# Parked output weights return after the q products, a fifth block of them is parked, and more of V stays on the chip

## The chip, the cores and the metric

The kernel runs on one core of a Trainium2 chip. The metric is device time in microseconds (us) of one execution. The core has the engines PE (TensorE, matrix products into PSUM), DVE (VectorE), ACT (ScalarE), POOL (GpSimd) and SP (SyncE, which issues the transfers from HBM). PEld is PE's loading of weights, which overlaps its products.

## The reference

Four residual layers over x of 4 x 1 x 512: attention, gated unit, attention, gated unit. Both attention layers use the same weights and caches, and so do both gated units.

```python
def _A_ref(x, k_cache, v_cache, wq, wo):          # Hq 32, Hkv 8, Dh 128, Sk 8192
    W = min(4096, max(256, Sk // 4))              # 2048: only the last 2048 keys count
    q = (x @ wq).reshape(B, Sq, Hq, Dh).transpose(0, 2, 1, 3)
    k = jnp.repeat(k_cache[:, :, Sk - W:, :], rep, axis=1)   # rep 4
    v = jnp.repeat(v_cache[:, :, Sk - W:, :], rep, axis=1)
    p = _softmax(jnp.einsum("bhqd,bhkd->bhqk", q, k) * (Dh ** -0.5), axis=-1)
    o = jnp.einsum("bhqk,bhkd->bhqd", p, v)
    return o.transpose(0, 2, 1, 3).reshape(B, Sq, Hq * Dh) @ wo

def _B_ref(x, w_gate, w_up, w_down):              # F 1792
    return (sigmoid(x @ w_gate) * (x @ w_up)) @ w_down

x = x + _A_ref(_layernorm(x), ...)
x = x + _B_ref(_layernorm(x), ...)
x = x + _A_ref(_layernorm(x), ...)
x = x + _B_ref(_layernorm(x), ...)
```

All inputs are bf16. K and V of the window are 16 MiB each.

## The kernel before

**Stages.** The layers are numbered 0 to 3. Layer 0 loads wq, K of all heads and V head by head. K is transposed on PE (L741) and copied back to its place by ACT and DVE (L751), so that layer 2 finds it on the chip. Per head: scores (L764), maximum (L773), exp (L786), a block transpose of the weights (L792, L797), their spreading over the four batches (DVE L822, in layer 2 also ACT L829), the reciprocal of their sum (L837, L841), the product with V (PV: L864 in the wide form, whose column groups L880 adds up, L922 in the plain form), its scaling (omul, L933) and the product with the head's rows of wo (L985, for the last heads L896 or L947). Layer 0 takes the heads in the order 1 to 6, 0, 7, layer 2 in the order 0 to 7. The gated units load w_up, w_gate (L1152) and w_down (L1228 in layer 1, L1225 in layer 3).

**Places.** On-chip memory is dealt out in units of 128 x 256 bf16 (64 KB over all partitions). The places are `arena` ("ar", 75 units), `wo_sb` ("ws", 64 units, 8 per head for wo), `kt` ("kt", 256 units, 32 per head for K), `side` ("sx") and the small `pb` and `pt`. The table `WHERE` gives each load its places. V of a head has 32 units. `VKEEP` names the unit from which V of a head stays on the chip between layers 0 and 2: for head 7 it is unit 26, so that six units are kept and 26 are loaded again. In layer 2, V of heads 2 to 7 goes to places in `kt` that K of heads 0 to 5 leaves free, each as soon as the scores of that head are done.

**Parking.** In layers 1 and 2 some units of `wo_sb` are wanted for other weights. `stash(0)` copies four blocks of four units (ws 8 to 23, DVE L1032) into PSUM banks 1, 2, 0 and 3. Then w_gate, a piece of w_down and two pieces of wq are loaded into these units. `stash(1)` copies the blocks back (ACT L1028). It stands ahead of `project_q` (L704, the q products of layer 2) in the program.

**Row sum's bank.** PSUM bank 7 (`WB`) gathers the wo products of most heads (L985): four strips of 32 rows, of which each strip's first 16 rows are written. It is set to zero once at the start. At the end of an attention layer ACT and DVE copy it as hi and lo parts (L998, L1004), and eight products with the 0/1 tile `ofbb` (L1011, w_turn) sum its rows and turn them; w_early (L1017) adds this to x.

**Order.** Each operation is entered with the tokens that it reads and writes, its PSUM banks and a planned time. `_schedule` places the operations of each engine by these planned times, `_assign_sync` adds the waits. So moving or adding an operation can change the order on the other engines. SP issues the transfers strictly in the order of the program, each once its places are free.

Of the kernel before, what the change touches and what calls it, by code (L numbers as in the profile page):

```python
# [268 lines left out]
def build(nc, A_x, A_k, A_v, A_wq, A_wo, B_wg, B_wu, B_wd, out):  # L269
# [3 lines left out]
    NB, SQ, D = A_x.shape  # L273
    _, HKV, SK, DH = A_k.shape
# [15 lines left out]
    NR = NB * REP  # L290
# [3 lines left out]
    WOH = REP * D  # L294
# [10 lines left out]
    AHEAD = 2  # L305
    NWR = {0: HKV - 1, 2: HKV - 2}
    WIDE = {0: {0: 4, 1: 4, 2: 4, 3: 4, 4: 4, 5: 4, 6: 2}, 2: {2: 2, 3: 2, 4: 2, 5: 2}}
    VKEEP = {0: 24, 7: 26}
    HEADS1 = list(range(1, HKV - 1)) + [0, HKV - 1]
    HEADS2 = list(range(HKV))  # L310

# [27 lines left out]
    with es:  # L339
# [3 lines left out]
        kt = sb("kt", [128, HKV * NB * BLK], BF16)  # L343
        wo_sb = sb("wo_sb", [128, HKV * WOH], BF16)
# [12 lines left out]
        pb = sb("pb", [128, 4 * UNIT], BF16)  # L357
# [4 lines left out]
        tin = sb("tin", [128, 32], F32)  # L362
# [9 lines left out]
        ofb, ofr = (lambda t: (t[:, 0:NB], t[:, NB:2 * NB]))(sb("ofbr", [128, 2 * NB], F32))  # L372
        onr = sb("onr", [128, 4 * NR], BF16)
# [3 lines left out]
        rowq, ofbb, ones_b = (lambda t: (t[:, 0:NR], t[:, NR:NR + NB], t[:, NR + NB:]))(sb("rqb", [128, NR + NB + 2], BF16))  # L377
# [16 lines left out]
        ps = es.enter_context(nc.psum_tensor("ps", [128, 8, 512], F32))  # L394
# [5 lines left out]
        P = _Plan()  # L400
# [9 lines left out]
        def blk_tok(s):  # L410
            return tuple((s[0], u) for u in range(s[1], s[1] + s[2]))
# [12 lines left out]
        def ar(u, n):  # L424
            return ("ar", u, n)

        def sx(u, n):
            return ("sx", u, n)

        WHERE = {}  # L430
        for n in range(HKV - 1):
            WHERE["V0_%d" % HEADS1[n]] = [ar(MAIN - UHEAD if n % 2 == 0 else 0, UHEAD)]
        WHERE["V0_%d" % (HKV - 1)] = [ar(0, 16), ar(16, 10), ar(30, 6)]
        WHERE["u01"], WHERE["g01"] = ar(52, 2 * GU), ar(38, 2 * GU)
        PT3 = ("kt", 187, 4)
        WHERE.update({
            "g23_1": ("ws", 8, 2 * GU), "u23_1": ar(0, 2 * GU),
            "d0_1": ar(14, 8), "d4_1": ar(22, 8), "d8_1": ar(36, 2), "d9_1": ("ws", 22, 2), "d10_1": ("pb", 0, 4),
            "d12_1": ("pt", 4, 4),
            "q01": [("ws", 8, 8), ar(0, 14), ar(14, 4), ("ws", 16, 6)],  # L440
            "V2_0": [ar(18, 12), ar(36, 2), sx(0, 8), sx(8, 2), ar(66, 8)],
            "V2_1": [sx(10, NS - 10), ar(0, 11)],
            "V2_6": [("kt", 128, 16), ("kt", 144, 16)],
            "V2_7": [("kt", 160, 16), ("kt", 176, 10), ar(30, 6)],
            "g23_3": ar(0, 2 * GU), "u23_3": sx(0, 2 * GU),
            "d0_3": ar(14, 8), "d4_3": ("kt", 192, 8), "d8_3": ("kt", 200, 8), "d12_3": sx(14, 4),
        })
# [7 lines left out]
        def c_dve(n, rate=None):  # L455
            return tm["dve_fix"] + n * (tm["dve_f32"] if rate is None else rate)
# [14 lines left out]
        def load_v(L, h):  # L471
# [3 lines left out]
            for s in WHERE["V%d_%d" % (L, h)]:  # L475
# [16 lines left out]
             r=[("ones_f",)], w=[("ident_f",)])  # L492
        P.op("gpsimd", "ident_b", 200.0, lambda g: g.tensor_copy(ident_r[:, :].rearrange("p (r x) -> p r x", r=4),
                                                                   ident_f[:, :].unsqueeze(1).broadcast_to([128, 4, 128])),
             r=[("ident_f",)], w=[("ident_b",)])
# [9 lines left out]
        def e_rowq(v):  # L505
            with nc.allow_low_precision("zeros and ones"):
# [8 lines left out]
             r=[("ident_f",)], w=[("perm",)])  # L515
        P.op("vector", "ofb", c_dve(128),
             lambda v: v.tensor_reduce(ofb[:, :], ident_f[:, :].rearrange("p (s b) -> p b s", b=NB), AXX, ALU.add),
             r=[("ident_f",)], w=[("ofb",)])
        P.op("vector", "ofr", c_dve(128),
             lambda v: v.tensor_reduce(ofr[:, :], ident_f[:, :].rearrange("p (r y) -> p r y", r=REP), AXX, ALU.add),  # L520
             r=[("ident_f",)], w=[("ofr",)])
        P.op("vector", "ofbb", c_dve(NB), lambda v: v.tensor_copy(ofbb[:, :], ofb[:, :]), r=[("ofb",)], w=[("ofbb",)])

        P.op("vector", "own", c_dve(16),
             lambda v: v.tensor_reduce(tin[:, 0:REP], rowq[:, :].rearrange("p (b r) -> p r b", b=NB), AXX, ALU.add),
             r=[("rowq",)], w=[("tin",)])
        P.op("vector", "same0", c_dve(32),
             lambda v: v.tensor_copy(tout[:, :], eye32[:, :]), r=[("eye32",)], w=[("tout",)])
        P.op("vector", "same1", c_dve(16),
# [2 lines left out]
             r=[("tin",), ("tout",)], w=[("tout",)])  # L532
        P.op("vector", "same2", c_dve(32),
             lambda v: v.tensor_scalar(same[:, :], tout[:, :], -1.0e30, 1.0e30, ALU.mult, ALU.add),
             r=[("tout",)], w=[("same",)])
# [3 lines left out]
        WB = 7  # L539
# [8 lines left out]
        def emit_xT_in(t):  # L548
            last = None
            for c in range(NC):  # L550
# [4 lines left out]
             w=[("psx",)], banks=(MB,))  # L555
        P.op("vector", "xT_cp", c_dve(NX), lambda v: v.tensor_copy(xT[:, :], bankb(MB)[:, 0:NX]),
             r=[("psx",)], w=[("xT",)], banks=(MB,))
# [134 lines left out]
        def project_q(L, pieces, pieces_last):  # L692
            if not L:
                return project_first(pieces, pieces_last)
            prev, toks, seen = [], {0: [], 1: []}, set()
            HB = HQ // 2
            for n, (ap, tk, ktc, q0, q1) in enumerate(pieces):
                on = sorted(set(q // HB for q in range(q0, q1)))
                first = [max(q0, i * HB) for i in on if i not in seen]
                seen.update(on)  # L700

                def e_q(pe, ap=ap, ktc=ktc, q0=q0, q1=q1, first=first):
                    for q in range(q0, q1):
                        last = pe.matmul(ps[:, QB + q // HB, q % HB * NB:(q % HB + 1) * NB],  # L704
                                         ap[:, (q - q0) * 128:(q - q0 + 1) * 128],
                                         xn[:, ktc * (NB + 1):ktc * (NB + 1) + NB],
                                         start=(q in first), stop=(ktc == pieces_last), skip_group_check=True)
                    return last
                prev = [P.op("tensor", "qproj%d_%d" % (L, n), tm["pe_pair"] * (q1 - q0), e_q,
                             r=list(tk) + [("xn",)], w=[("psq", n)], banks=tuple(QB + i for i in on), order=prev)]  # L710
                for i in on:
                    toks[i].append(("psq", n))
            mc = means(L, tq, cs_q, HQ)
            for i in range(2):
                tv = tq[:, i * HB * NB:(i + 1) * HB * NB]
                P.op("vector", "q_mean%d_%d" % (L, i), c_dve(HB * NB),
                     lambda v, i=i, tv=tv: v.tensor_tensor(tv, ps[:, QB + i, 0:HB * NB], tv, ALU.subtract),
                     r=toks[i] + [mc], w=[("qm", i)], banks=(QB + i,))
                P.op("vector", "q_evac%d_%d" % (L, i), c_dve(HB * NB),
                     lambda v, i=i, tv=tv: v.tensor_tensor(  # L720
                         qs[:, 28:28 + HKV * NB * STRIP].rearrange("p (h b s) -> p h b s", h=HKV, b=NB)[:, 4 * i:4 * i + 4, :, 0:REP],
                         tv.rearrange("p (h r b) -> p h b r", h=HKV // 2, r=REP),
                         rstd[:, :].unsqueeze(1).unsqueeze(3).broadcast_to([128, HKV // 2, NB, REP]), ALU.mult),
                     r=[("qm", i), ("rstd",)], w=[("qs1",)] if i else [("qs",)])
# [177 lines left out]
        def pv_wo(L, n, h, pbk, pieces, prev=()):  # L902
# [8 lines left out]
            for s, j0 in () if wide else pieces:  # L911
                def e_pv(pe, s=s, j0=j0):
                    last = None
                    j1 = j0 + s[2] * UNIT // 128
                    for j in range(j0, j1):
# [13 lines left out]
                             r=blk_tok(s) + pk + (("pa", kp),), w=[("pso", obk, j0)], banks=(obk,), order=prev)]  # L929
# [12 lines left out]
            if n == HKV - 1:  # L942
                def e_wo(pe):
                    last = None
                    for c in range(NC):
# [7 lines left out]
                     r=[("wo", h), ("on", k2)], w=[("psl", obk)], banks=(obk,))  # L953
# [28 lines left out]
            def e_wo(pe):  # L982
                last = None
                for j in range(4):
                    last = pe.matmul(ps[32 * j:32 * j + NR, WB, 0:D], onr[:, j * NR:(j + 1) * NR],  # L985
                                     wo_sb[:, h * WOH + j * D:h * WOH + (j + 1) * D],
                                     start=(n == 0), stop=(n == NWR[L] - 1), skip_group_check=True)
                return last
# [29 lines left out]
                 r=[("pswt",), ("xT",)], w=[("xT",)], banks=(MB,))  # L1018

        GB, UB, YB = 0, 1, 2  # L1020
        STASH = ((8, 3), (12, 0), (16, 1), (20, 2))

        def stash(back):
            for u, b in STASH if back else STASH[1:] + STASH[:1]:
                at = blk_ap(("ws", u, 4))
                r, w = [("wo", u * UNIT // WOH)], [("st", b)]
                if back:
                    P.op("scalar", "back%d" % u, 1010.0, lambda a, b=b, at=at: a.copy(at, bankb(b)), r=w,  # L1028
                         w=r + list(blk_tok(("ws", u, 4))), banks=(b,))
                else:  # L1030
                    P.op("vector", "stash%d" % u, 620.0,
                         lambda v, b=b, at=at: v.tensor_scalar(ps[:, b, :].bitcast(I32), at.bitcast(I32), 0, None, ALU.bitwise_or),  # L1032
                         r=r, w=w + [("pst", b), ("pss", b)] + list(blk_tok(("ws", u, 4))), banks=(b,))

        gkeep = {}

# [94 lines left out]
        def glu(L, last_layer):  # L1131
# [76 lines left out]

            parts = [(fc, min(NFC, fc + 4)) for fc in range(0, NFC, 4)]
            if not last_layer:  # L1210
                parts[2:] = [(8, 9), (9, 10), (10, 12), (12, 14)]
            for fc0, fc1 in parts:
                s = load_d(L, fc0, fc1)

# [101 lines left out]
        for w in WHERE["q01"]:  # L1316
# [6 lines left out]
                    streamed.append((blk_ap(t), blk_tok(t), ktc, q0, q1))  # L1323
            u0 += w[2]
        assert u0 == HQ
        stash(1)
        project_q(2, kept_q + streamed, 1)
        vs2 = {}
        SB2, TB2 = [3, 0], [1, 2]

# [10 lines left out]
        turns = []  # L1341
        for n, h in enumerate(HEADS2):
            turns.append(scores(2, n, h, SB2[n % 2], TB2[n % 2]))
            if n + 1 < HKV:
                vs2[HEADS2[n + 1]] = load_v(2, HEADS2[n + 1])
            if n >= AHEAD:
                v2_head(n - AHEAD)
            weights(2, n, h, TB2[n % 2])
# [67 lines left out]
```

## Time and profile before

| | |
|---|---|
| median of 3 runs | 174.94 us (174.22 to 174.97) |
| profiled execution | 174.91 us |
| its span | 173.2 us |
| mean granted clock of PE | 0.819 |
| PE, DVE, ACT, POOL busy | 78%, 58%, 44%, 4% |
| read from HBM | 69.08 MB, 399 GB/s over the span |

The page of the profile has the busy shares of the engines, the span in 40 slices with the granted clock of PE (`PEclk`, tenths of full speed), the share of the 16 transfer rings that is busy (`DMA`) and the GB/s, then the queues and the chain of work that ended last. Beside the page there are views of the trace: the chain of waits in order of time, the timeline of single instructions, the transfers with the time from issue to landing, and the busy times by windows. A bracket at the end of a line of the timeline gives the engine's idle time before it and what ended that. Times in the trace count from the start of the span.

### The profile page before, as it was taken

Reading aid. Unit: us, or ns where it says so; the run is one execution under the profiler, and the core shown is the slowest. Engines: PE = TensorE matmul, PEld = TensorE weight load, DVE = VectorE, ACT = ScalarE, POOL = GpSimd, SP = SyncE. Lnnn points to the kernel's source line nnn. Section 1 sums busy time; section 2 is a strip of 40 time slices with the busy share of each in tenths; the row PEclk is TensorE's granted clock in tenths of the full one; section 3 lists DMA queues with packets and bytes.
Section 4 is the critical chain, followed back from the end, with each engine's and each line's share of the span. In section 5 each row is a group of like instructions: output and inputs, shape, how many; then the busy total and the mean of one; then the engine's idle time right before and its main releaser. Section 6 shows DMA issues by size and latency. Waiting matters only on the chain.

```text
span 173.2 us, 4888 instructions
## 1 busy us (share of the span) xinstructions
PE 135.6 (78%) x2178; PEld 98.5 (57%) x2178; DVE 100.0 (58%) x251; ACT 76.4 (44%) x133; POOL 7.0 (4%) x18
## 2 busy tenths in 40 slices
PE   0394599899798778997988785757887999868894
PEld 0292298657466465564764465756523766556782
DVE  7444015986838677695697643114187988854260
ACT  2064208848477547466292122023524644564110
POOL 5200000000000000000000000200200000100020
PEclk9999656999999999999999655555576999985555
DMA  5999999999999999999999999999999999999970
GB/s 183 424 429 418 417 424 431 424 408 446 428 412 429 407 433 435 409 437 419 429 415 418 395 391 411 409 393 413 414 432 435 422 416 414 420 418 419 413 310 29
DMA packets 9648, 69.39 MB, mean 401 GB/s; under 512 B 1048, under 2 KB 2204, under 8 KB 6172
## 3 DMA queue, kind: packets, MB, share of 16 engines
q1 hardware_dynamic: 9620, 69.08, 96.2%
q8 instruction: 17, 0.28, 0.6%
q14 instruction: 3, 0.02, 0.0%
q10 hardware_dynamic: 8, 0.00, 0.0%
HBM read 69.08 MB, written 0.00 MB: 399 GB/s over the span
## 4 chain that ended last, share of the span: by engine, by line
DMA 57%; PE 28%; DVE 6%; ACT 5%; issue 1%; SPq 1%; DVEq 0%; ACTq 0%
DMA arena<-in_A_v_cache_dram 32%; DMA kt<-in_A_v_cache_dram 11%; DMA arena<-in_A_wq_dram 10%; PE ps L764 5%; PE ps L864 5%; DMA wo_sb<-in_A_wq_dram 4%; PE ps L1152 4%; PE ps L741 4%; PE ps L673 2%; PE ps L922 2%; ACT pb L786 1%; ACT pt L829 1%; ACT wo_sb L1028 1%; PE ps L1225 1%; SPq L464 1%
## 5 line engine op out<-in xcount | busy, mean ns | idle before, releaser
L751 ACT COPY kt<-ps 128x1024 bf16<-128x1024 bf16 x40 | 39.1, 1018 | 26.0 <-PE ps L741 25.8
L741 PE MATMUL ps<-ident_r,kt 128*128 128x128 bf16 x512 | 38.6, 232 | 4.9 <-DMA kt<-in_A_k_cache_dram 2.7
L741 PEld LDWEIGHTS ps<-ident_r,kt 128*128 128x128 bf16 x512 | 33.1, 106 | 11.7 <-issue 4.4
L751 DVE COPY kt<-ps 128x1024 bf16<-128x1024 bf16 x24 | 29.2, 1215 | 12.9 <-PE ps L741 12.7
L764 PE MATMUL ps<-kt,qs 128*32 128x512 bf16 x256 | 19.3, 426 | 1.7 <-ACT pb L786 1.0
L822 DVE TENSOR_TENSOR pt<-ps,ofbr 128x1024 bf16<-128x1024 f32 (+1 forms) x15 | 15.5, 1030 | 3.3 <-PE ps L797 3.2
L864 PE MATMUL ps<-arena,pt 128*64 128x512 bf16 (+1 forms) x128 | 13.4, 391 | 4.6 <-DMA arena<-in_A_v_cache_dram 4.6
L773 DVE TENSOR_REDUCE nmz<-ps 128x1 f32<-128x512 f32 x16 | 11.0, 687 | 6.4 <-PE ps L764 6.3
L792 DVE STREAM_TRANSPOSE pb<-pb 128x512 bf16<-128x512 bf16 x16 | 11.3, 708 | 5.0 <-ACT pb L786 4.9
L786 ACT ACTIVATE pb<-ps,nmz 128x512 bf16<-128x512 f32 x16 | 11.1, 694 | 5.8 <-DVE nmz L783 5.7
L829 ACT ACTIVATE pt<-ps,ofbr 128x96 bf16<-128x96 f32 x28 | 7.2, 341 | 10.3 <-PE ps L797 10.3
L864 PEld LDWEIGHTS ps<-arena,pt 128*64 128x64 bf16 (+1 forms) x128 | 6.0, 117 | 10.1 <-DMA arena<-in_A_v_cache_dram 6.0
L764 PEld LDWEIGHTS ps<-kt,qs 128*32 128x32 bf16 x256 | 5.9, 102 | 8.0 <-ACT pb L786 1.9
L873 ACT COPY arena<-ps 128x512 f32<-128x512 f32 (+1 forms) x7 | 3.9, 555 | 14.1 <-PE ps L864 14.1
L837 PE MATMUL ps<-rowf,nmz 128*128 128x16 f32 x32 | 6.7, 285 | 2.8 <-DVE pt L822 2.6
L837 PEld LDWEIGHTS ps<-rowf,nmz 128*128 128x128 f32 x32 | 5.2, 203 | 5.8 <-DVE pt L822 4.1
L880 PEld LDWEIGHTS ps<-arena 128*128 128x128 f32 x52 | 6.7, 201 | 2.1 <-ACT arena L873 1.6
L880 PE MATMUL ps<-arena 128*128 128x16 f32 x52 | 7.4, 273 | 0.7 <-ACT arena L873 0.2
L1152 PE MATMUL ps<-xn,arena 128*128 128x5 bf16 (+1 forms) x168 | 6.2, 172 | 2.0 <-DMA arena<-in_B_w_up_dram 1.1
L1152 PEld LDWEIGHTS ps<-xn,arena 128*128 128x128 bf16 x168 | 6.2, 118 | 2.2 <-DMA arena<-in_B_w_up_dram 1.2
L1028 ACT COPY wo_sb<-ps 128x1024 bf16<-128x1024 bf16 x4 | 4.0, 1012 | 7.6 <-DMA wo_sb<-in_A_wq_dram 7.5
L635 POOL TENSOR_TENSOR rs<-pt,rs 128x4 f32<-128x4 f32 x3 | 3.0, 1015 | 107.0 <-DVE pt L631 107.0
(165 smaller groups left out, 159.9 us busy)
## 6 DMA issues: line engine op xcount, KB each, us to landing
kt<-in_A_k_cache_dram SPq DMA_DIRECT2D x8, 2048.0 KB, 24.7
arena<-in_A_v_cache_dram SPq DMA_DIRECT2D x7, 2048.0 KB, 20.3
kt<-in_A_v_cache_dram SPq DMA_DIRECT2D x3, 2048.0 KB, 14.6
kt<-in_A_v_cache_dram SPq DMA_DIRECT2D x5, 1024.0 KB, 18.5
wo_sb<-in_A_wo_dram SPq DMA_DIRECT2D x8, 512.0 KB, 25.4
kt<-in_A_wq_dram SPq DMA_DIRECT2D x1, 2048.0 KB, 11.7
side<-in_A_wq_dram SPq DMA_DIRECT2D x1, 1984.0 KB, 15.8
arena<-in_B_w_up_dram SPq DMA_DIRECT2D x2, 896.0 KB, 7.8
```

Of the source, the lines that this page charges most:

```text
L741: last = pe.transpose(bankb(bank)[:, (v * NB + q) * 128:(v * NB + q + 1) * 128], kt[:, c0:c0 + 128], ident_b[:, :])
L751: return (e.tensor_copy if ev == "vector" else e.copy)(to, fr)
L764: last = pe.matmul(ps[32 * b:32 * b + 32, sbk, 0:CB * 128], qs[:, q0:q0 + 32], blk_ap(kblk(h, b))[:, c * CB * 128:(c + 1) * CB * 128], sta ...
L773: lambda v: v.tensor_reduce(nmv, ps[:, sbk, 0:CB * 128], AXX, ALU.max, negate=True),
L786: o = a.activation(pbuf[:, :], ps[:, sbk, 0:CB * 128], ACTF.Exp, bias=gv, scale=1.0, accum_out=zv)
L792: P.op("vector", "ptr%d_%d" % (L, h), 650.0, lambda v: v.transpose(turned[:, :], pbuf[:, :]), r=[("pb", 0), ("pb", 1)], w=[("pb", 2), ("pb ...
L822: lambda v: v.tensor_tensor(pv4[:, 0:nj], spread(tbk, nj).unsqueeze(2).broadcast_to([128, nj, NB, REP]), ofb[:, :].unsqueeze(1).unsqueeze( ...
L829: last = a.mul(pv4[:, nj:NJ4, b, :], spread(MB, NJ4 - nj), ofb[:, b:b + 1])
L837: lambda pe: pe.matmul(ps[:, tbk, CB * NQ:CB * NQ + NR], zv.broadcast_to([128, 128]), rowf[:, :], start=True, stop=True),
L864: last = pe.matmul(ps[rows * g:rows * (g + 1), bank, 0:wide * 128].rearrange("p (c d) -> p c d", c=wide), ptv[:, w0:w0 + rows], v, start=( ...
L880: last = pe.matmul(ps[:, out[0], out[1]:out[1] + NR], part[:, c * 128:(c + 1) * 128], ey[wide][:, c * NR:(c + 1) * NR], start=(c == 0), st ...
L1152: last = pe.matmul(ps[:, bank, fc * wid:(fc + 1) * wid], cols[:, fc - g0, :], xn[:, ktc * (NB + 1):ktc * (NB + 1) + wid], start=(ktc == 0 ...
```

## The change

1. `VKEEP` of head 7 goes from 26 to 22: ten units of its V are kept in `arena` (26 to 35) between the attention layers, and 22 are loaded again. In both layers the second piece of V of head 7 has 6 units, and the third, kept one has 10.
2. A fifth block of four units (ws 24 to 27) is parked in bank 7 after the row sum of layer 0 has been read from it, and comes back behind the exp of the first head of layer 2.
3. `stash(1)` stands behind `project_q`. The q products of layer 2 thus read the wq pieces in `wo_sb` as they were loaded, and the copies back wait for these products; before, the copies came between the loads and the products.
4. Since bank 7 now holds parked weights in all rows, the first wo product of layer 2 writes 32 rows of the first three strips, and one more product starts the fourth strip; `ofbb` is made from a 0/1 tile (`own`) whose ones stand only at the rows that count.
5. The places of w_down in layer 1 (pieces of 4, 3, 1, 2, 2 and 2 row blocks instead of 4, 4, 1, 1, 2 and 2), of wq in layer 2 (three pieces instead of four) and of the first V of layer 2 move.

The order that results on the engines: in layer 0 PE has 44 PV products of head 7 ahead of w_turn and 20 behind it (32 and 32 before). In layer 2 the scores of head 0 stand behind all q products (before: ahead of the last 12), and those of heads 0 to 2 stand together; for head 7, 20 products with kept V, 32 with the first loaded piece and 12 with the second (12, 32 and 20 before). DVE has one instruction more (the fifth parking, behind L1004), ACT one more copy, which stands behind the first exp of layer 2. Further on ACT has the exp of head 3 ahead of the spreading of head 2.

```diff
-    VKEEP = {0: 24, 7: 26}
+    VKEEP = {0: 24, 7: 22}
...
-        WHERE["V0_%d" % (HKV - 1)] = [ar(0, 16), ar(16, 10), ar(30, 6)]
+        WHERE["V0_%d" % (HKV - 1)] = [ar(0, 16), ar(16, 6), ar(26, 10)]
...
-            "d0_1": ar(14, 8), "d4_1": ar(22, 8), "d8_1": ar(36, 2), "d9_1": ("ws", 22, 2), "d10_1": ("pb", 0, 4),
+            "d0_1": ar(14, 8), "d4_1": ("ws", 22, 6), "d7_1": ar(36, 2), "d8_1": ar(22, 4), "d10_1": ("pb", 0, 4),
             "d12_1": ("pt", 4, 4),
-            "q01": [("ws", 8, 8), ar(0, 14), ar(14, 4), ("ws", 16, 6)],
-            "V2_0": [ar(18, 12), ar(36, 2), sx(0, 8), sx(8, 2), ar(66, 8)],
+            "q01": [("ws", 8, 10), ar(0, 14), ("ws", 18, 8)],
+            "V2_0": [ar(14, 12), ar(36, 2), sx(0, 8), sx(8, 2), ar(66, 8)],
...
-            "V2_7": [("kt", 160, 16), ("kt", 176, 10), ar(30, 6)],
+            "V2_7": [("kt", 160, 16), ("kt", 176, 6), ar(26, 10)],
...
-        P.op("vector", "ofbb", c_dve(NB), lambda v: v.tensor_copy(ofbb[:, :], ofb[:, :]), r=[("ofb",)], w=[("ofbb",)])
...
+        P.op("vector", "ofbb", c_dve(NB), lambda v: v.tensor_copy(ofbb[:, :], tin[:, 0:NB]), r=[("tin",)], w=[("ofbb",)])
...
                 for j in range(4):
-                    last = pe.matmul(ps[32 * j:32 * j + NR, WB, 0:D], onr[:, j * NR:(j + 1) * NR],
+                    rows = 2 * NR if L and n == 0 and j < 3 else NR
+                    if L and n == 0 and j == 3:
+                        pe.matmul(ps[96:128, WB, 0:D], onr[:, 2 * NR:4 * NR], wo_sb[:, h * WOH:h * WOH + D], start=True,
+                                  stop=False, skip_group_check=True)
+                    last = pe.matmul(ps[32 * j:32 * j + rows, WB, 0:D], onr[:, j * NR:j * NR + rows],
...
-        STASH = ((8, 3), (12, 0), (16, 1), (20, 2))
-
-        def stash(back):
-            for u, b in STASH if back else STASH[1:] + STASH[:1]:
+        STASH = ((8, 3), (12, 0), (16, 1), (20, 2), (24, WB))
+
+        def stash(back, at_last=False):
+            for u, b in (STASH[4:] if at_last else STASH[:4]) if back else STASH[1:4] + STASH[:1] + STASH[4:]:
                 at = blk_ap(("ws", u, 4))
                 r, w = [("wo", u * UNIT // WOH)], [("st", b)]
                 if back:
                     P.op("scalar", "back%d" % u, 1010.0, lambda a, b=b, at=at: a.copy(at, bankb(b)), r=w,
-                         w=r + list(blk_tok(("ws", u, 4))), banks=(b,))
+                         w=r + list(blk_tok(("ws", u, 4))), banks=(b,),
+                         order=[o for o in P.ops if o.name == "sexp2_%d" % HEADS2[0]])
                 else:
                     P.op("vector", "stash%d" % u, 620.0,
                          lambda v, b=b, at=at: v.tensor_scalar(ps[:, b, :].bitcast(I32), at.bitcast(I32), 0, None, ALU.bitwise_or),
-                         r=r, w=w + [("pst", b), ("pss", b)] + list(blk_tok(("ws", u, 4))), banks=(b,))
+                         r=r, w=w + [("pst", b), ("pss", b)] + list(blk_tok(("ws", u, 4))) + [("psw", n) for n in range(HKV)] * (b == WB),
+                         banks=(b,))
...
-                parts[2:] = [(8, 9), (9, 10), (10, 12), (12, 14)]
+                parts[1:] = [(4, 7), (7, 8), (8, 10), (10, 12), (12, 14)]
...
-        stash(1)
-        project_q(2, kept_q + streamed, 1)
+        project_q(2, kept_q + streamed, 1)
+        stash(1)
...
             turns.append(scores(2, n, h, SB2[n % 2], TB2[n % 2]))
+            if n == 0:
+                stash(1, True)
```

## The prediction

> **What bounds the kernel now.** I read the page first (clock, transfers, chain), then the chain of waits in order of time, then the timeline of the last stage, the transfers with their time to landing, and the windows over the end.
>
> The page: granted clock and transfer share in 40 slices of 4.33 us, queues, chain by engine.
> ```profile
> PEclk9999656999999999999999655555576999985555
> DMA  5999999999999999999999999999999999999970
> ...
> q1 hardware_dynamic: 9620, 69.08, 96.2%
> q8 instruction: 17, 0.28, 0.6%
> ...
> DMA 57%; PE 28%; DVE 6%; ACT 5%; issue 1%; SPq 1%; DVEq 0%; ACTq 0%
> ```
> The transfers are busy from the first slice to the last but two. 69.08 MB must come in, and the engines work in their shadow.
>
> The chain of waits, in order of time (start, us, what):
> ```profile
> 111.90 7.61 DMA wo_sb<-in_A_wq_dram
> ...
> 119.54 1.02 ACT wo_sb L1028
> ...
> 120.58 1.02 ACT wo_sb L1028
> ...
> 121.65 1.56 PE ps L704 x52
> ...
> 143.17 18.37 DMA kt<-in_A_v_cache_dram
> ...
> 161.58 0.73 PE ps L922 x20
> ```
> The copies back (L1028) do stand on this chain, but the chain then goes through a transfer issued at 143.17 that lands only 18.37 us later: it had stood in a long queue. What the engines win before that gets the last V in no sooner.
>
> The transfers (times, KB, us from issue to landing) and the end of the timeline:
> ```profile
> kt<-in_A_v_cache_dram SPq DMA_DIRECT2D x1, 640.0 KB, 18.4
> ...
> pb<-in_B_w_down_dram SPq DMA_DIRECT2D x1, 256.0 KB, 10.2
> pt<-in_B_w_down_dram SPq DMA_DIRECT2D x1, 256.0 KB, 10.4
> ```
> ```profile
> 161.58 0.61 PEld L922 LDWEIGHTS ps<-kt 128*128 128x128 bf16 x20 [0.40 <-DMA kt<-in_A_v_cache_dram]
> 161.58 0.72 PE L922 MATMUL ps<-kt 128*128 128x32 bf16 x20 [0.30 <-DMA kt<-in_A_v_cache_dram]
> ...
> 169.63 0.34 PEld L1225 LDWEIGHTS ps<-kt,pt 128*25 128x25 bf16 x16 [0.18 <-DMA kt<-in_B_w_down_dram]
> 170.26 0.13 PEld L1225 LDWEIGHTS ps<-side,pt 128*25 128x25 bf16 x8 [0.29 <-DMA side<-in_B_w_down_dram]
> 170.26 0.40 PE L1225 MATMUL ps<-side,pt 128*25 128x128 bf16 x8
> ```
> The last 20 PV products wait for the last V, and the last two groups of the down projection wait for the last weights (0.18 and 0.29 us). So the end is set by the last landing, near 170.2; PE alone could be 0.47 us (0.18 + 0.29) earlier.
>
> The windows over the end (us; busy of PE, PEld, DVE, ACT, POOL; clock; transfer share; GB/s):
> ```profile
> 166.00:166.50 0.50, 0.50 (x21) 0.50 (x19) 0.32 (x2) 0.00 (x0) 0.50 (x1) 0.50 1.04 393
> ...
> 169.50:170.00 0.50, 0.50 (x27) 0.34 (x16) 0.00 (x0) 0.00 (x0) 0.00 (x0) 0.50 0.21 61
> ```
> The 16 rings do not end together: the share falls from 1.04 to 0.21 over 3.5 us. The slowest ring sets the last landing.
>
> **The change part by part.** The profiled execution took 174.91 us (span 173.2 and 1.71 around it), 0.03 under the median 174.94.
>
> Bytes. V of head 7 is streamed in the second attention layer for 22 units instead of 26; four units of 128 x 256 bf16 are 262,144 bytes. From 140 to 160 us the windows show 419, 410, 419 and 417 GB/s, mean 416: 0.63 us. The other sizes change, their sum does not. The Trainium skill (DMA: Bandwidth & Descriptors, section Bandwidth) puts the HBM side at about 358 GB/s per core; by that figure the bytes would be 0.73 us, an estimate, and the sum 0.1 lower; the trace sustains 416 here and decides.
>
> One transfer fewer (wq in three pieces, not four). The pb and pt pieces, issued at 107.33 and 107.81, land at 117.53 and 118.21: 0.68 apart, where 256 KB at 416 GB/s are 0.63. So about 0.05 us each; between 0 and 0.1, I take 0.05.
>
> Sum on the transfers: 0.63 + 0.05 = 0.68 us, all before or at V of head 7, so each later landing moves by that.
>
> PE at the end. The 32 products at 160.27 end at 161.28; now the last piece lands near 160.9, so the wait of 0.30 goes. Twelve products follow instead of 20: 8 x 0.036 (0.72 / 20) = 0.29 less. The eight move to the kept group (near 157.2), ahead of the second half of head 6; that half landed just before its products start at 157.55, with the row sum (L837, 0.61) now written earlier, so I take nothing for them; at worst 0.29 comes back. PE gains 0.59 (0.30 at worst), and had 0.47 to spare: 1.06 (0.77) against 0.68. The transfers stay last.
>
> The fifth parking (stash24, DVE). The nearest row is the fourth, 0.67 us at 97.84. It must follow w_lo (L1004, ends 104.45) and goes 104.46 to 105.13. Queued behind it on DVE are w_early (was 104.99, 0.14 later) and omul0_7, which waits for PE until 105.86. PE now does 12 of the later 32 PV products ahead of w_turn, in its idle 0.54 us before 104.60, so omul0_7 comes about 0.35 sooner. None of it lasts: the next stages wait for u and w_down transfers (113.00, then 114.76 to 118.28). Without that cover it would cost 0.67.
>
> SP's queue. The second w_down piece now goes to parked places and waits for stash24 (105.13); w_down began at 105.54 before, so that is no later. Behind it stand the other w_down pieces and wq. The last wq piece waits for the second w_down group's products (about 116.1; was issued at 115.75), and the first V of layer 2 for the fourth's (about 117.2; was 116.24). These land 7.6 and 9.4 us after issue, queued behind others, so a delay of 0.4 to 1.0 is hidden: 0.
>
> Copies back. Before, two (119.54 to 121.60) held the first wq products, and two (123.38 to 125.44) the last 12. Now products wait for landings alone; the last landing stays near 115.75 + 7.6 = 123.35, as the bytes up to there are the same. S of head 0, now behind all q products on PE, starts near 123.9, as before (123.89), so the place for V of head 2 comes free at 125.83 again. Even if not: the V pieces issued at 123.02 and before land up to 9.7 us after that, so the rings have work to 132.7, and a slip of a few us starves none; past that each us would count in full. Copies of units 16 and 20 run to about 126.0 on ACT; the exp of head 0 began at 127.67, so 1.7 us cover them. The fifth copy (1.01) follows that exp, 128.45 to 129.47; the weights of head 0 (L829) began at 129.73: covered by 0.26, and with no cover at most 1.01 on head 0. The first WO of the layer has one product more, about 0.15 us (0.60 / 4). ACT takes exp of head 3 ahead of the weights of head 2 (0.69 + 0.19 later at worst). All this is ahead of PV waits on transfers at 150.10, 152.58 and 155.21; the weights for the last were ready at 151.79, 3.4 us early. So 0.
>
> Setup (ofbb from another tile): the same DVE instruction one place later, near 3.4 us, where the first K is still on its way: 0. The other transfers that were cut anew (V of head 7 in layer 0, w_down, first V of layer 2) keep their number and bytes: 0. Total: 174.91 - 0.68 = 174.23.
>
> **The rivals.**
>
> Forecast: the last landing moves by 0.68, 174.2. For it: the waits at 161.58, 169.63 and 170.26. Own range 173.9 to 174.6.
>
> A ring step, either way. The page counts 17 instruction fetches, 0.28 MB, so 16.5 KB each; a ring moves 416 / 16 = 26 GB/s, so each fetch delays its ring by 0.63 us. One more or fewer on the slowest ring makes 174.9 or 173.6. For it: rings that end 3.5 us apart, and the three runs (174.97, 174.94, 174.22), which differ by about one such step.
>
> PE becomes the bound. If the longer kept group pushes head 6's half and the later chain so that PE gains nothing, only the spare 0.47 is won: 174.44. It decides once PE gains under 0.21; my worst was 0.30.
>
> Slower: the half clock. The clock is 0.5 from 98 to 127, 1.0 for one stretch, 0.5 again from 131 to 134, then 1.0. S at half takes 1.90 per head, 1.05 at full; 32 PV products of L864 1.90 against 1.24. So a head loses about 1.5 us, or some 1.7 us in 3.4 us of PE work. If the changed order keeps the clock at half through three further such stretches after 134, 5.1 us are lost against the 3.4 of cover at head 6: 174.23 + 1.7 = 175.9. Up to two stretches it costs nothing. For it: PE drops back at 131; against: S of heads 0 to 2 now stand together, so PE idles less there. The Trainium skill (TensorE: Matmul & The Clock Gate, Part 1) says that half rate is the default, that about 3.4 us of sustained activity releases it, and that the window runs free, so that the phase differs from run to run. By that rule the drop at 131 could be longer or absent; the trace agrees as far as a drop of about 3 us goes.
>
> The change does not do what it says: the kept places overwritten and V streamed anyway would be 174.9; the written transfers show 384 KB, so next to nothing.
>
> **How the numbers follow.** A measurement of this kernel tells about 0.5%, 0.87 us: under 174.07 is faster, over 175.81 slower. Forecast 0.50, of which 0.20 below 174.07; ring step down 0.20 (faster), up 0.10 (same); PE bound 0.12 (same); clock 0.08 (slower). Faster 0.40, same 0.30 + 0.10 + 0.12 = 0.52, slower 0.08. The range goes from 173.5 (a step, and the upper price of the dropped transfer) to 175.0 (the step up); it leaves out the clock and the tails.
>
> **What would show it.** Right: 68.8 MB in q1; the last V transfer 384 KB, landing near 160.9, 12 products after it with no wait; the last w_down landing near 169.6, still waited for; no L1028 in the chain; rate unchanged. Wrong: a slice of transfers under 9 between 20 and 160 us; PE not waiting at the end; a half clock from 134 to 150; S of head 0 well after 123.9.

## The result, and the profile after

The changed kernel takes 174.17 us in the median of 22 runs (173.62 to 175.15), the kernel before 174.75 beside it (174.21 to 175.29). The ratio is 0.9971, with a 95% interval of 0.9959 to 0.9984: faster by 0.3%, less than one measurement of this kernel tells from no change. The forecast was 174.2. The profiled execution took 174.00 us, 0.91 under the one before, which is more than the medians moved (0.58). One run further down, of pad448 with 176.92 us, was in a slow state and is left out of its median.

From the page: granted clock and transfer share in 40 slices, the two queues, the chain by engine.
```profile
PEclk9999656999999999999999755555567899995555
DMA  5999999999999999999999999999999999999980
...
q1 hardware_dynamic: 9476, 68.82, 96.4%
q8 instruction: 17, 0.28, 0.6%
...
DMA 53%; PE 31%; DVE 9%; ACT 3%; issue 2%; SPq 1%; DVEq 0%; ACTq 0%
```
0.26 MB less in q1, the same number of instruction fetches, no slice under 9 between the first and the last two. But the transfers' share of the chain fell from 57% to 53%, and PE's and DVE's rose. The chain of waits, in order of time (start, us, what), shows where:
```profile
116.81 6.81 DMA wo_sb<-in_A_wq_dram
123.67 0.59 PE ps L703 x16
...
149.53 0.40 PE ps L836 x2
...
160.07 1.21 PE ps L921 x44
```
No copy back (L1031 now) is left in it, and no transfer either after 123.67: the last V, which carried 18.37 us of the chain before, is gone from it. From the products of q to the end, 46 us, the chain is engines alone in this profile. It is close: V of head 5 landed at 149.52, only 0.33 before its products began (149.85), and in a second profile of the same kernel (control, below) the chain goes through that landing.

The end of the timeline (start, us, engine, line and operation; in brackets the wait before it and what ended it):
```profile
157.21 0.93 PEld L921 LDWEIGHTS ps<-pt,kt 128*128 128x128 bf16 x32 [0.15 <-DMA kt<-in_A_v_cache_dram]
...
159.93 1.33 PE L921 MATMUL ps<-kt 128*128 128x32 bf16 x44
...
168.19 0.13 PEld L1230 LDWEIGHTS ps<-arena,pt 128*25 128x25 bf16 x7 [0.34 <-issue]
...
169.35 0.13 PEld L1230 LDWEIGHTS ps<-side,pt 128*25 128x25 bf16 x8 [0.19 <-DMA side<-in_B_w_down_dram]
169.36 0.40 PE L1230 MATMUL ps<-side,pt 128*25 128x128 bf16 x8
```
The 32 and 12 products of head 7 run as one group of 44 with no wait (0.30 before). The last group waits 0.19 for its weights (0.29 before), and a new stall of 0.34 stands in the middle of the first group of the down projection, put down to no releaser. The last V transfer, among the transfers (KB, us from issue to landing), and the windows over the end (us; busy of PE, PEld, DVE, ACT, POOL; clock; transfer share; GB/s):
```profile
kt<-in_A_v_cache_dram SPq DMA_DIRECT2D x1, 384.0 KB, 17.2
```
```profile
166.00:166.50 0.50, 0.50 (x21) 0.50 (x19) 0.22 (x1) 0.17 (x1) 0.00 (x0) 0.50 0.72 287
...
169.00:169.50 0.50, 0.50 (x27) 0.30 (x15) 0.00 (x0) 0.00 (x0) 0.00 (x0) 0.50 0.12 33
```
The queue thins out 0.9 us sooner: 0.72 at 166 where it was 1.04, and the last landing, by the records of the landings, is 169.32 (170.23 before).

### The profile page after: what moved, and what is told of

Same layout as the page of the kernel before. It is cut to its first block, busy times and chain, and to the rows that moved or that the text cites. A ratio compares the mean times of both kernels' runs of the same rounds, so it can differ in the third digit from the quotient of the medians.

```text
span 172.3 us, 4893 instructions
## 1 busy us (share of the span) xinstructions
PE 134.8 (78%) x2179; PEld 98.2 (57%) x2179; DVE 100.9 (59%) x252; ACT 77.3 (45%) x134; POOL 7.0 (4%) x18
## 3 DMA queue, kind: packets, MB, share of 16 engines
q1 hardware_dynamic: 9476, 68.82, 96.4%
HBM read 68.82 MB, written 0.00 MB: 400 GB/s over the span
## 4 chain that ended last, share of the span: by engine, by line
DMA 53%; PE 31%; DVE 9%; ACT 3%; issue 2%; SPq 1%; DVEq 0%; ACTq 0%
DMA arena<-in_A_v_cache_dram 32%; DMA arena<-in_A_wq_dram 10%; DMA wo_sb<-in_B_w_down_dram 7%; PE ps L863 6%; PE ps L763 6%; DMA wo_sb<-in_A_wq_dram 4%; PE ps L921 4%; PE ps L740 4%; PE ps L1157 2%; PE ps L672 2%; PE ps L836 2%; DVE pt L821 2%; DVE nmz L772 2%; ACT pb L785 1%; PE ps L1230 1%
## 5 line engine op out<-in xcount | busy, mean ns | idle before, releaser
L1031 ACT COPY wo_sb<-ps 128x1024 bf16<-128x1024 bf16 x5 | 5.0, 1011 | 9.0 <-PE ps L703 9.0
L634 POOL TENSOR_TENSOR rs<-pt,rs 128x4 f32<-128x4 f32 x3 | 3.0, 1015 | 106.5 <-DVE pt L630 106.5
```

## The experiments

Theory T is that of the prediction: transfers set the end, and the time follows their bytes and number. O: the order of products and copies brings the gain. P: since the change the engines alone set the end. F: the instruction fetches set it, through the slowest ring. E, formed from drop6: engines and last landing are now equally late. R, beside it: what holds drop6 is a wait that neither the bytes nor the products touch. The kernels were run in groups, each with its own runs of the kernel before, so the last column but one is what to compare; the interval is that of the ratio to the kernel before.

| kernel | median us | before beside it | difference | ratio, interval |
|---|---|---|---|---|
| after | 174.17 | 174.75 | -0.58 | 0.9971, 0.9959 to 0.9984 |
| control (after again) | 174.23 | 174.65 | -0.42 | 0.9969, 0.9948 to 0.9989 |
| keep6 | 174.82 | 174.82 | 0.00 | 0.9990, 0.9970 to 1.0011 |
| keep0 | 175.69 | 174.82 | +0.87 | 1.0049, 1.0031 to 1.0066 |
| split13 | 175.32 | 174.65 | +0.67 | 1.0041, 1.0024 to 1.0059 |
| drop6 | 174.23 | 174.82 | -0.59 | 0.9970, 0.9950 to 0.9989 |
| short_pe | 173.99 | 174.77 | -0.78 | 0.9948, 0.9932 to 0.9964 |
| drop6_short | 173.27 | 174.77 | -1.50 | 0.9913, 0.9894 to 0.9933 |
| cutq7 | 173.90 | 174.77 | -0.87 | 0.9952, 0.9933 to 0.9971 |
| reorder_only | 174.74 | 174.65 | +0.09 | 0.9997, 0.9978 to 1.0015 |
| copies_first | 175.95 | 174.82 | +1.13 | 1.0065, 1.0043 to 1.0088 |
| pad448 | 174.55 | 174.77 | -0.22 | 0.9983, 0.9965 to 1.0001 |
| pad784 | 185.84 | 174.65 | +11.19 | 1.0611, 1.0574 to 1.0649 |

The changed kernel stands at -0.58 and -0.42; the others are set against -0.5.

**The bytes: keep6 and keep0.** Fewer units of V of head 7 kept, all else as changed.
```diff
-    VKEEP = {0: 24, 7: 22}
+    VKEEP = {0: 24, 7: 26}      # keep6; keep0: VKEEP = {0: 24}
...                              # keep6: the places of its pieces follow (16, 10 and 6 units)
```


> The changed kernel with one part undone: V of head 7 keeps 6 units again (26 are streamed in the second attention layer), with the fifth parking, the moved copies and the longer pieces left in. Theory T (the last landing sets the end, and it follows the bytes): four units of 64 KB more, 262,144 bytes at 416 GB/s = 0.63 us, so 174.17 + 0.63 = 174.80, which is the kernel before less the one transfer that is saved. Rival O (the gain comes from the order of products and copies, or from fewer products behind the last V): 174.2 to 174.4, since only the bytes go back. Written transfers 69.08 MB, last V piece of 640 KB landing 0.6 later than after's 160.64.

> The changed kernel with V of head 7 keeping nothing: all its 32 units are streamed in the second attention layer, 10 units and no further transfer than those two (16 units each) more. Theory T: 655,360 bytes at 416 GB/s = 1.58 us, so 175.75, and if the last piece has 16 products behind it instead of 12, nothing more, because the weights still land last. Rival O: under 0.5 us more. Rival E (engines behind the last V set the end): 1.58 plus up to 0.15 for four products more behind the last landing.

keep6 is back at the kernel before (0.00): +0.5 for four units, 0.63 expected. keep0 is +1.4 for ten (1.58 expected). keep0 brings V of head 7 in pieces of 16, 6 and 10 units, which is one transfer more than its expectation says, so the 1.4 holds that too. keep6 also has 20 products behind the last V again, but they don't set its end: behind them PE waits for the last weights as in the kernel before (0.28 and 0.29).
```profile
170.27 0.13 PEld L1230 LDWEIGHTS ps<-side,pt 128*25 128x25 bf16 x8 [0.28 <-DMA side<-in_B_w_down_dram]
```
So the gain is the bytes of the four units, not the parking or the order around them. That both cost less than their bytes fits a changed kernel that no longer gains all that its transfers save (drop6, below). The Trainium skill (DMA: Bandwidth & Descriptors, section Bandwidth) gives 358 GB/s for a core when both cores of its HBM domain read. By that figure keep0 would be 1.83, an estimate; the measured 1.4 is on the other side of 1.58.

**The number of transfers: control and split13.** V of heads 2 to 6 in pieces of 8 units.
```diff
-            WHERE["V2_%d" % h] = [("kt", (h - 2) * UHEAD, UHEAD)]
+            WHERE["V2_%d" % h] = [("kt", (h - 2) * UHEAD + 8 * i, 8) for i in range(4)]
...                              # heads 5 and 6 in the same way
```


> The changed kernel as it is, for the other runs of this chip: 174.17, 0.58 us under the kernel before.

> The changed kernel with V of heads 2 to 6 of the second attention layer brought in pieces of 8 units each, with the same bytes: thirteen transfers more. Theory T with the price of a transfer as the prediction took it (0.05 us each): 0.65 us slower, 174.8; at the ends of its bounds, 0 and 0.1 us each, 174.2 to 175.5. If the queue hides a transfer's own cost altogether: no change.

+1.1 to +1.2, so 0.09 us for each of 13 transfers: inside the bounds of 0 and 0.1, near the upper one. In its profile the last landing is 170.96, 1.64 later than in the changed kernel's, and 0.58 of that stood ahead of the first cut piece (last wq piece at 124.21 for 123.63): 1.06 is left for the 13. Not all of it need be the transfers' own price, since PE's order changes with it too.

**Fewer bytes still: drop6.** One transfer is left out.
```diff
+                if (L, h, u0) != (2, 7, 16):
                     dma("V%d_%d_%d" % (L, h, u0), ...)
```


> The changed kernel without the transfer of the 6-unit second piece of V of head 7 in the second attention layer; its products are still made, with what stands in those places. Theory T: 393,216 bytes at 416 GB/s and one transfer fewer, 0.94 + 0.05 = 0.99 us sooner for each landing behind it, 173.2, as far as PE lets it: the trace of after shows PE waiting for w_down only 0.19 us at the end, against 0.47 before. Rival P (PE has become as late as the transfers): 0.2 to 0.5 us sooner, 173.7 to 174.0, with no wait on a transfer left in the last stage.

Nothing: -0.59 against -0.58 and -0.42. T's 0.99 failed, and so did the 0.2 to 0.5 of its rival P. The timeline of drop6 (its lines are one higher) has no wait for a transfer after 149.82:
```profile
159.93 1.25 PE L922 MATMUL ps<-kt 128*128 128x32 bf16 x44
...
168.16 0.13 PEld L1231 LDWEIGHTS ps<-arena,pt 128*25 128x25 bf16 x7 [0.40 <-issue]
168.18 0.96 PEld L1231 LDWEIGHTS ps<-kt,pt 128*25 128x25 bf16 x32
...
168.99 0.36 PEld L1231 LDWEIGHTS ps<-side,pt 128*25 128x25 bf16 x8
```
The 44 products start at 159.93 as in the changed kernel, and the last weights load without a wait. The last transfer in the chain of drop6 is the first piece of V of head 5, which was queued ahead of the transfer left out:
```profile
133.28 16.50 DMA kt<-in_A_v_cache_dram
```
In control it is the same piece (issued at 133.06, landed at 149.46, its products from 149.51). So what stands level with the last landing is the engines' work from about V of head 5 on, and no byte saved behind that V can start it sooner. Upward the time follows the bytes, downward no more: the changed kernel stands on the corner.

**Both sides of the corner: short_pe and drop6_short.**
```diff
-                    for fc in range(NFC):
+                    for fc in range(1 if last_layer and ktc == 2 else NFC):
```


> The changed kernel with TensorE work left out behind the last V: of the 28 gate and up products of the last layer that read the third slice of the input, 26 are not made (their sums lack that slice); all transfers as before. At half clock 84 such products take 2.72 us, so 26 x 0.032 = 0.84 us. Theory E (since the change the engines' chain and the last landing are equally late, so neither alone moves the end): 0 to 0.2 us sooner, since PE waited only 0.19 us for the last weights; 174.0 to 174.2, and the wait for w_down grows to about 1 us. Rival P (the engines alone set the end): 0.84 sooner, 173.4.

> Both cuts together: the 6-unit second piece of V of head 7 is not brought in the second attention layer (its products read what stands there) and the 26 gate and up products of the last layer are left out. Theory E (equally late): each alone gives next to nothing, both together the smaller of the two, 0.84 us, 173.4. Rival P (engines alone): the same as the shortened products alone. Rival R (what holds drop6 is neither, but a wait that neither cut touches): 174.2 again.

Bytes alone gave 0 to 0.2, products alone 0.2 to 0.4, both together 0.9 to 1.1 (-1.50 against -0.58 and -0.42). That is E; P would have given short_pe its 0.84 whole, and R would have held drop6_short at 174.2. Not all of the 0.9 to 1.1 need be the 26 products (0.84): drop6_short also lacks a stall of PE in the down projection that drop6 has (0.40, see below). In the timeline of short_pe what the products won has become waits for w_down:
```profile
166.93 0.37 PEld L1230 LDWEIGHTS ps<-arena,pt 128*25 128x25 bf16 x16 [0.85 <-DMA arena<-in_B_w_down_dram]
...
168.75 0.34 PEld L1230 LDWEIGHTS ps<-kt,pt 128*25 128x25 bf16 x16 [0.91 <-DMA kt<-in_B_w_down_dram]
```

**Where the engines' chain begins: cutq7.** Seven eighths of the last wq piece stay away, ahead of the whole layer.
```diff
-            dma("wq2_%d" % u0, blk_ap(w), wq_d[:, 0, u0 * UNIT:(u0 + w[2]) * UNIT], w=blk_tok(w),
+            got = 1 if u0 == 24 else w[2]
+            dma("wq2_%d" % u0, blk_ap((w[0], w[1], got)), wq_d[:, 0, u0 * UNIT:(u0 + got) * UNIT], w=blk_tok(w),
...                              # the planned time stays that of the whole piece
```


> The changed kernel with the last piece of the query weights of the second attention layer cut from 8 units to 1 in its transfer (the products read what stands in the other seven places); no other instruction changes. 7 units are 458,752 bytes, 1.10 us at 416 GB/s, ahead of everything of that layer. Theory E, with the engines' chain beginning at the products of q, which wait for that piece (landing 123.63): both chains come sooner, 1.0 to 1.1 us, 173.1, where the 0.99 us that drop6 took out behind V of head 5 gave nothing. Rival (the chain that holds drop6 begins somewhere else, in the exps or the copies that wait for no transfer): under 0.4 us.

Against the changed kernel -0.3 to -0.45, with intervals that overlap, so the expectation of 1.0 failed, and what there is lies about the rival's bound of 0.4. The timeline of cutq7 around q:
```profile
119.03 0.38 PE L1233 MATMUL ps<-pt 128*128 128x4 bf16 x8 [0.30 <-DMA pt<-in_B_w_down_dram]
...
123.57 0.57 PE L703 MATMUL ps<-xn,wo_sb 128*128 128x4 bf16 x16
...
124.07 0.26 DVE L719 TENSOR_TENSOR qs<-pt,rs 128x64 bf16<-128x64 f32 x1
...
124.48 0.62 PE L763 MATMUL ps<-kt,qs 128*32 128x512 bf16 x4 [0.35 <-DVE pt L716]
```
The products of q wait for no wq any more (0.32 in the changed kernel, at 123.67). But they begin only at the residual of layer 1, behind the last w_down landing (119.03 here, 118.66 there), and at half clock PE needs until 123.7 for the others of them and the norm's sums; L716 and L719 on DVE follow. S of head 0 starts at 124.48, no sooner than the 124.19 of the changed kernel; counted from the first products of q it is 4.80 us for 4.88, so hardly any of the 0.32 came through. V of head 5 lands at 149.55 (149.52), PE waits for it, and the chain starts from there as in drop6. So the 1.10 us didn't reach the point from which the engines set the end; if the 0.3 to 0.45 of the medians is more than noise, its cause is open. Since V of head 2 is issued behind S of head 0, the bytes saved became a hole in the queue. Windows of cutq7, and then of the changed kernel (last column GB/s):
```profile
122.00:124.00 2.00, 2.00 (x68) 1.97 (x67) 0.39 (x2) 1.08 (x2) 1.01 (x1) 0.50 0.97 347
124.00:126.00 2.00, 1.65 (x21) 0.76 (x22) 0.66 (x3) 1.97 (x3) 0.00 (x0) 0.50 0.83 249
```
```profile
122.00:124.00 2.00, 1.68 (x59) 1.55 (x56) 0.59 (x3) 1.45 (x2) 1.01 (x1) 0.50 1.07 393
124.00:126.00 2.00, 2.00 (x30) 0.91 (x31) 0.49 (x2) 1.97 (x3) 0.00 (x0) 0.50 1.02 405
```
2 x (46 + 156) = 404 KB less moved in these 4 us, 0.97 us at 416 GB/s, of the 1.10 saved.

**The order: reorder_only and copies_first.** The first is the kernel before with the products of q ahead of the copies back; the second is the changed kernel with the copies ahead again.
```diff
-        project_q(2, kept_q + streamed, 1)
         stash(1)
+        project_q(2, kept_q + streamed, 1)      # copies_first; reorder_only the other way round
```


> The kernel before with one part of the change alone: the products of q of the second attention layer ahead of the copies of the parked units. Theory T: the same bytes and transfers, so as the kernel before, 174.75 within 0.15. Rival O (the order brings the gain): 174.2 or less.

> The changed kernel with one part undone: the copies of the parked units stand ahead of the products of q of the second attention layer again (the products then read what the copies leave in those places, so part of q is another matrix's product; the work is the same). Theory T: the products wait for the copies, S of head 0 starts about 2 us later than 124.2, and the queue has transfers until about 132, so 174.17 within 0.15. Rival O (the order decides): 1 to 2 us slower, up to 176.

Alone the new order gives nothing (+0.09). But with wq cut into the changed kernel's three pieces, the old order costs 1.55 to 1.7 us. The last wq piece lands at 123.80 in places that copies overwrite, a copy of 1.01 starts only then (123.81), and the last 64 products follow; S of head 0 starts at 127.00. Windows of copies_first, whose profiled run (176.79) is 0.84 over its median, and then of the changed kernel:
```profile
128.00:130.00 2.00, 2.00 (x28) 0.61 (x16) 0.98 (x3) 0.00 (x0) 0.00 (x0) 0.61 0.96 324
130.00:132.00 2.00, 0.85 (x20) 0.34 (x16) 1.66 (x5) 1.52 (x3) 0.00 (x0) 1.00 1.01 335
```
```profile
128.00:130.00 2.00, 1.26 (x18) 0.45 (x18) 1.73 (x5) 1.62 (x5) 0.00 (x0) 1.00 1.03 430
130.00:132.00 2.00, 0.81 (x10) 0.44 (x14) 1.92 (x5) 1.53 (x6) 0.00 (x0) 0.84 1.09 455
```
V of head 2 was issued at 128.94 instead of 126.14, and less moved meanwhile, 324 and 335 GB/s for 430 and 455, though the share still reads about 1. So the order is what the recut pieces need, not a gain by itself.

**The fetches: pad784 and pad448.**
```diff
+        def e_pad(g):
+            for c in range(2 * NFC):
+                for p in range(0, 128, 32):
+                    last = g.memset(csum[p:p + 32, HQ + c:HQ + c + 1], 0.0)
+            return last
+        for i in range(7):      # pad784; pad448: range(4)
+            P.op("gpsimd", "pad%d" % i, 6000.0, e_pad, w=[("cs",), ("mhalf",)])
```


> The changed kernel with 784 small memsets on the idle POOL engine ahead of the first attention layer's streaming, for their instructions alone: about 50 KB, three instruction fetches of 16.5 KB more. Theory F (a fetch delays the ring that carries it by 16.5 KB at 26 GB/s = 0.63 us, and the slowest ring sets the end): from 0 to +1.9 us by which rings take them, one step of 0.63 likeliest; 20 fetches in the profile. Rival (fetches share all rings' time): 3 x 16.5 KB at 416 GB/s = 0.12 us.

> The changed kernel with 448 small memsets on the idle POOL engine (784 of them took 100.9 us and made the norm of the MLP wait; 448 should end near 82 us, ahead of it). Their instructions come by a queue of their own: 784 raised its fetches from 3 to 9 and its bytes from 0.02 to 0.07 MB, so 448 should make about 6 and 0.05 MB. Theory F (a fetch delays its ring by its bytes at 26 GB/s: 8 KB are 0.3 us, and the slowest ring sets the end): 0 to 0.9 us slower by which rings take them. Rival (fetches share all rings, or fall into the slack of rings that are ahead): within 0.1 us of 174.2.

pad784 says nothing of fetches: its memsets took 100.9 us on POOL from first to last, the norm of the MLP (L634) came only at 125.48, and the transfers stood still behind it. Nor did q8 move; POOL's instructions come by q14 (3 to 9 fetches). pad448 ended its memsets at 82 us and took q14 from 3 to 7 fetches and from 0.02 to 0.06 MB: +0.3 (+0.20 and +0.36 by the two runs of the changed kernel), with intervals that overlap. It leans to F and doesn't settle it.

## Why the prediction was right, and where its steps were not

**The sum on the transfers held.** 0.63 for the bytes and 0.05 for the transfer were to give 0.68; the medians give 0.58 and 0.42, the last landing 0.91 in one profile. In these 0.91, V of head 7 shows a part that is chance: the first piece, of unchanged size, landed 0.33 sooner (160.00 to 159.67) on the slowest ring, while its fastest ring was 0.06 later. The second piece followed its first by 0.97 instead of 1.54: 0.57 by size alone. A transfer is worth 0.09 by split13 rather than 0.05.

**The step that was mis-sized is PE's spare.** "PE gains 0.59 ... and had 0.47 to spare: 1.06 (0.77) against 0.68" left PE 0.38 (0.09 at worst) ahead of the transfers. In the profile it is 0.19, in that of control the last weights aren't waited for at all, and drop6 shows that nothing more was to be had: about 0 in the medians. PE did gain, 1.03 at the start of the glu products (163.45 to 162.42), more than I gave it: PV of head 5, which waited for its V before, started 0.25 sooner (150.10 to 149.85), the waits of 0.33 and 0.30 went or shrank, and eight products fewer follow. But 0.34 came back in the stall at 168.19. It stands after the ninth of 16 weight loads in after, control, drop6, cutq7 and pad448 (0.34, 0.36, 0.40, 0.63, 0.21), and ends at 168.16 to 168.43 in all five, though PE came to this group between 167.29 and 167.98. By the records of the transfers, a fetch of 16 KB of instructions (q8) starts 2.52 to 2.63 us before that end in each of the five (at 165.67 in the changed kernel). In the kernels that come to the group after 168.6 the tenth load is 2.60 us or more behind that fetch: before, keep6 and reorder_only have no stall there, keep0 and split13 pause for about 0.2. short_pe and drop6_short have 26 products fewer ahead of it, and there the tenth load comes 1.72 and 1.61 us behind the fetch without a stall, as if the fetched instructions began further on in the program. So the fetch fits as the cause, but no run moved it alone, and it is not shown. "PE becomes the bound" was given 0.12 and 174.44: in the medians it is a tie, with the forecast's time. The sum held because PE just kept up; that it did so with nothing to spare, where the prediction had counted 0.38, is luck.

**The covers.** "The rings have work to 132.7" was wrong as a measure of slack, and it didn't matter only because S of head 0 came at 124.19, 0.3 after the forecast. Here the slack counted on the ring that ran out first, and ended when the next transfer began to move, not when it was issued. By the landings of copies_first, the fastest ring had its last piece at 130.23 and V of head 2 (2 MB, 4.90 us in the changed kernel) at 136.36, so by that rate it stood 1.23 us idle: V issued at 128.94 needed 2.52 us before it counted. This is an estimate, from one profile. With it, the changed kernel's own cover is 129.48 - (126.14 + 2.52) = 0.82 us, not the 6.9 that I had (132.7 less 125.83). copies_first spent it and lost the rest. The Trainium skill (DMA: Bandwidth & Descriptors, section Latency and other measured facts) gives an HBM access 2 us at high load; the 2.52 is of that order, but what makes it up no run here shows.

The other covers held. The fifth parking ended at 104.96 and the first w_down piece into it landed at 116.25, which PE waited for; but as the chain shows, the last wq piece, issued at 116.81 (116.1 forecast), landed later than the products behind that wait needed it, by 0.32. The fifth copy took 128.35 to 129.35, and the weights of head 0 began at 129.74 (129.73 before). The changed kernel's chain passes through no copy, in either profile.

**The rivals.** "The change does not do what it says" fell with 384 KB and 68.82 MB. The slower rival, the half clock, did not come: the clock was half from 131.4 to 134.8 (131.0 to 134.4 before). In cutq7 this stretch is missing and PV of head 4 starts 0.66 sooner (139.33 for 139.99), but PE then waits for V of head 5 at 149.59: the gain ends in the cover. By the Trainium skill (TensorE: Matmul & The Clock Gate, Part 1) the window runs free and the phase differs from run to run. Two runs of the changed kernel agree: one is at half clock from 155.2 to the end, the other (control) from 152.2 to 159.0 and again from 162.4, with full clock between.

The ring step can be seen once. In the profile of pad448 (175.36 us, median 174.55) one of the 16 rings lands the last three w_down pieces 0.97 us behind all others: at 168.81 where the next latest is 167.84, then 170.05 after 169.07 and 170.66 after 169.69. One piece earlier the latest two were 166.60 and 166.54. PE waits for these pieces:
```profile
170.09 0.34 PEld L1230 LDWEIGHTS ps<-kt,pt 128*25 128x25 bf16 x16 [0.91 <-DMA kt<-in_B_w_down_dram]
170.70 0.13 PEld L1230 LDWEIGHTS ps<-side,pt 128*25 128x25 bf16 x8 [0.27 <-DMA side<-in_B_w_down_dram]
```
Between the level piece and the first late one a fetch by q8 ran, from 165.84 to 166.92; the fetches added for POOL were over by 82. In the changed kernel's profile a ring in the middle loses 1.0 or more at the same place, and the last landing doesn't move. So a step is nearer 1 us than 0.63, and counts if the slowest ring takes it. That the fetch makes it is a coincidence in time, not a test.

## What to carry to other kernels

When a kernel is bound by transfers, price a saving by the bytes, and then ask how much of it the next limit leaves: count every wait that the saving would remove, from the first one on, since what stands behind them (here the engines' work from about V of head 5 to the end) becomes the bound when they are gone. A kernel tuned against one limit stands close to several: test the corner from both sides, with one cut, the other, and both. Count the cover in a queue on its fastest ring, and less what a transfer takes to start (2.5 us by the one estimate here).

## What the runs showed of the hardware

- The transfer share can read about 1 while much less moves (0.96 and 1.01 at 324 and 335 GB/s, in copies_first); it fell to 0.83 only at 249 GB/s (cutq7). Look for a hole in GB/s.
- Instructions are fetched by queues of their own: padding POOL raised q14 from 3 to 9 fetches and left q8 at 17. 784 memsets of 32 cells took 100.9 us on POOL, 0.129 each, of which it was busy 0.091.
- The same transfer lands on the 16 rings over about 3 us: the first piece of V of head 7 from 156.51 to 160.00 before and from 156.57 to 159.67 after. The last landing is that of one ring, and it differs from run to run (pad448, above).
